# Attention with rotary embedding and two gated MLPs in fp32 on one core: key tails open each P times V accumulation, two P times V groups per pair, issue order of all stages redone

## The chip, the core and the metric

One core of a Trainium2 chip runs the whole program. The metric is device microseconds of one execution. TensorE is called PE here, its weight load PEld, VectorE DVE, ScalarE ACT, GpSimd POOL, SyncE (which issues most DMAs) SP.

## What is computed

The reference, cut to what matters (q, k, v are 4 x 8 x 576 x 64; `rotate` is the rotary embedding):

```python
q_rot, k_rot = (rotate(q), rotate(k))
scores = 1.0 / np.sqrt(D) * np.matmul(q_rot, k_rot.transpose(0, 1, 3, 2))
scores = scores - np.max(scores, axis=-1, keepdims=True)
attn = np.exp(scores)
attn = attn / (np.sum(attn, axis=-1, keepdims=True) + 1e-09)
x = np.matmul(attn, v)          # then heads side by side: 2304 x 512
x = (1.0 / (1.0 + np.exp(-(x @ w_gate))) * (x @ w_val)) @ w_out      # d_ff 1536
h = x @ w_in
return (h * (1.0 / (1.0 + np.exp(-1.702 * h)))) @ w_out2             # d_ff 2048
```

## The kernel before

The program has two stages. The first is attention over 16 pairs of heads (4 batches, 4 pairs each). The second is both MLPs, in chunks of 256 hidden columns; it begins when the last pair's output is there. Numbers keep nearly the whole of fp32: a value is split into a high part and a remainder, and products of both are summed.

For one pair of heads the first stage does this:

- **Load and rope.** `load` (L240) brings q and k of both heads, transposed. `rope_mul` (L275, four multiplications of 128x576, POOL, two of pair 1 on DVE) and `rope_add` (L282, two additions of 128x576, c = 0 and 1) make the rotated values. `split_qk` rounds each half on ACT (L291) and subtracts on DVE (L294); `stack` then copies halves between partitions by six DMAs (L364). Pair 0 has a path of its own (`rope_first`, L266 and L268; PE transposes, L333; copies, L341, L345 and L441). Pair 1 has L316 and L320 in place of L291 and L294.
- **Scores.** `scores` makes nine units of a pair: four row blocks of 128 queries for each of two heads, and one unit of the 64 last queries of both heads (the tail). Each unit is four matmuls of 288 columns (L385, L386), the tail unit four more and six of 64 rows. DVE takes the row maximum from PSUM (`nm`, L388); ACT takes exp with the row sum (`exps`, L403), into tiles P (five buffers) and Pt. Score PSUM has two buffers.
- **Transposes.** `transpose_p` turns P by PE (L457, L467, L472), up to four transposes of 128x128 into one of three PSUM buffers, and copies them to the tile PT on DVE (L441) where the step's number stands in `PT_DVE`, otherwise on ACT (L443).
- **Normalising.** `inverse` sums and inverts (L415, L416 on DVE) and spreads on POOL (L418, L421); `spread` turns that by PE (L428, L430) and copies it to a tile R.
- **P times V.** The queries of a pair are two pieces, a = 0 (256 columns) and a = 1 (320 columns). For each piece `pv` sums over the keys into the one PSUM buffer `ps_x`: for each of four key blocks two matmuls, one for each head, which write 64 partitions each (L488), and one matmul of all 128 partitions for the 64 key tails of both heads (L485, with `vtail`). The profile counts two records for each of these fp32 matmuls. When the sum is closed, DVE multiplies it by R into `xf` (L511). Only then can the next piece open the buffer.

The order of issue is written out by hand. `slot(G)` issues all steps that are due in slot G, and pair i's scores unit u stands in slot 9i + u. The tables before `dec = []` give each step a lag against slot 9i: `PT`, `INV`, `SPREAD`, `PV`, and, counted backwards, `ROPE_MUL`, `ROPE_ADD`, `ROPE_T` and the loads. The last pair has its own row. `slot` also fixes which kind of step comes first within a slot, and `PV_EARLY` names the steps of P times V that stand before the slot's scores. Slots below `FILL` = 20 don't exist: `FIRST` lists the steps of the filling one by one. `DEC` places the decoding of the first weight chunk (L170 to L188), whose high halves are split from raw 8-byte words on ACT, DVE and POOL; `SPLIT` places the splitting of the attention's output (`split_x`, L105 and L106). Each engine works through its own list in order, and a wait holds up all that stands behind it.

In the steady part before the change, a pair's piece a = 0 is issued in two groups of PE work (two key blocks, a scores unit and more, then the two others and the key tails) and piece a = 1 in a third, with its key tails some units later.

Of the kernel before, what the change touches and what calls it, by code (L numbers as in the profile page):

```python
# [31 lines left out]
def attention_then_mlps(  # L32
# [443 lines left out]
    def pv(i, a, ts):  # L476
# [3 lines left out]
        if ts[0] == 0:  # L480
            st[i]["pv"] = ps_t.tile([P, 512], F32, tag="pv", name="ps_x", bufs=1)
        ps = st[i]["pv"]
        for t in ts:
            if t == MAINC:
                nc.tensor.matmul(ps[:, :n], st[i]["vtail"], PT[:, MAINC, :], start=False, stop=True)  # L485
                continue
            for h in range(2):
# [422 lines left out]
```

## Time and profile before

| | |
|---|---|
| three runs | 1144.54, 1144.92 and 1146.52 us, median 1144.92 |
| profiled execution: its own time, its span | 1143.05 us, 1141.0 us |
| busy over the span | PE 98%, PEld 81%, DVE 69%, ACT 37%, POOL 21% |
| attention stage, MLP stage | until about 300 us, from there to the end |
| granted clock of TensorE, mean of the span | 1.000 |

The page of the profile names the share of the span in which each engine is busy, and the chain that ended last: each piece of it is the work that released the next. Where PE's busy time equals the stretch it has no idle time that the records show, though a matmul's end is modelled, so a PE that looks busy can still hide short stalls. The distance from one start to the next is then the better measure. DVE's instructions overlap a little at their ends, so that the sum of their durations can exceed the busy time.

### The profile page before, as it was taken

How to read it: one execution, taken by the hardware profiler on the slowest of the kernel's cores; microseconds unless marked ns; L12 is line 12 of the kernel's file. 1: busy time of each engine (PE TensorE's matmuls, PEld its weight loads, DVE VectorE, ACT ScalarE, POOL GpSimd, SP SyncE). 2: the span in 40 equal slices, each digit the busy share in tenths (PEclk: the TensorE clock that was granted, in tenths of full speed). 3: DMA queues.
4: the chain of work that ended last, by engine and by line, in shares of the span. 5: the costliest groups of instructions: out<-in, count | busy, mean ns of one | idle time of the engine just before them, and what ended most of it. 6: DMA issues, size and time to landing. Idle time of an engine off the chain costs nothing.

```text
span 1141.0 us, 15592 instructions
## 1 busy us (share of the span) xinstructions
PE 1114.4 (98%) x6008; PEld 923.2 (81%) x6008; DVE 785.0 (69%) x1321; ACT 422.6 (37%) x872; POOL 241.0 (21%) x216
## 2 busy tenths in 40 slices
PE   5899999999999999999999999999999999999998
PEld 3677777778788888888888888888888888888887
DVE  5999899897686645656556454666767667676744
ACT  4677777777542211212112123332222222222221
POOL 4544444431331100101001013430101100010100
PEclk9999999999999999999999999999999999999999
DMA  5676656552311111111111010111111111111014
GB/s 175 172 205 153 195 166 171 159 131 52 107 60 38 56 37 38 56 37 54 37 39 46 29 42 34 38 37 37 56 38 41 52 38 37 37 56 38 19 37 129
DMA packets 36409, 85.03 MB, mean 75 GB/s; under 512 B 6640, under 2 KB 11888, under 8 KB 34544
## 3 DMA queue, kind: packets, MB, share of 16 engines
q1 hardware_dynamic: 35232, 83.05, 25.1%
q10 hardware_dynamic: 1104, 1.00, 0.3%
q8 instruction: 47, 0.77, 0.3%
q14 instruction: 26, 0.21, 0.1%
HBM read 60.44 MB, written 4.72 MB: 57 GB/s over the span
## 4 chain that ended last, share of the span: by engine, by line
PE 93%; DVE 5%; ACT 1%; issue 1%; DMA 1%; POOL 0%; ACTq 0%; DVEq 0%
PE psh L519 42%; PE pso L519 30%; PE ps_x L488 5%; PE ps_p L457 4%; PE pss L385 4%; PE pss L386 3%; PE ps_x L485 1%; DVE nm L388 1%; PE psh L541 1%; DVE Y L294 1%; DVE x L282 1%; PE ps_p L472 1%; PE ps_r L428 0%; DVE PT L441 0%; ACT P L403 0%
## 5 line engine op out<-in xcount | busy, mean ns | idle before, releaser
L519 PE MATMUL psh<-xhl,w_in 128*128 128x512 f32 (+1 forms) x2352 | 493.3, 367 | 0.0
L519 PEld LDWEIGHTS psh<-xhl,w_in 128*128 128x128 f32 x2352 | 410.4, 189 | 73.8 <-ACT sg L549 0.2
L549 ACT ACTIVATE sg<-psh 128x512 f32<-128x512 f32 (+1 forms) x140 | 77.6, 554 | 354.2 <-PE psh L519 353.5
L519 PE MATMUL pso<-w_out,g 128*128 128x512 f32 (+1 forms) x870 | 202.5, 388 | 0.0
L519 PEld LDWEIGHTS pso<-w_out,g 128*128 128x128 f32 x870 | 162.1, 188 | 33.1
L551 DVE TENSOR_TENSOR gf<-psh,sg 128x512 f32<-128x512 f32 (+1 forms) x140 | 89.0, 636 | 141.9 <-PE psh L519 95.4
L552 ACT ACTIVATE g<-gf 128x512 fp32r<-128x512 f32 (+1 forms) x140 | 82.5, 589 | 244.6 <-DVE gf L551 242.2
L553 DVE TENSOR_TENSOR g<-gf,g 128x512 fp32r<-128x512 f32 (+1 forms) x140 | 97.3, 695 | 91.8 <-ACT g L552 91.8
L519 PE MATMUL pso<-g,w_out 128*128 128x512 f32 (+1 forms) x720 | 152.8, 368 | 0.0
L519 PEld LDWEIGHTS pso<-g,w_out 128*128 128x128 f32 x720 | 125.8, 189 | 22.6
L188 POOL TENSOR_TENSOR w_in<-wt,w_in 128x512 fp32r<-128x512 f32 x38 | 50.1, 1319 | 370.0 <-DVE w_in L183 362.5
L388 DVE TENSOR_REDUCE nm<-pss 128x1 f32<-128x576 f32 x144 | 108.1, 752 | 25.2 <-PE pss L386 23.2
L403 ACT ACTIVATE P<-pss,nm 128x576 f32<-128x576 f32 x128 | 95.0, 742 | 51.2 <-DVE nm L388 30.9
L275 POOL TENSOR_TENSOR x<-x,rope_sb 128x576 f32<-128x576 f32 x57 | 88.9, 1573 | 71.3 <-DMA x<-in_qk_dram 57.8
L615 DVE TENSOR_TENSOR acc<-pso,acc 128x512 f32<-128x512 f32 (+1 forms) x127 | 83.4, 682 | 20.0 <-PE pso L519 17.7
L188 POOL TENSOR_TENSOR w_out<-wt,w_out 128x512 fp32r<-128x512 f32 x28 | 36.2, 1294 | 267.5 <-DVE w_out L183 265.0
L457 PE MATMUL ps_p<-ident,P 128*128 128x128 f32 x576 | 84.9, 275 | 1.5 <-DVE PT L441 0.8
L598 DVE TENSOR_TENSOR acc<-pso,acc 128x512 f32<-128x512 f32 (+1 forms) x100 | 61.6, 635 | 28.7 <-PE pso L519 28.7
L457 PEld LDWEIGHTS ps_p<-ident,P 128*128 128x128 f32 x576 | 69.4, 143 | 8.6 <-ACT P L403 1.2
L488 PE MATMUL ps_x<-PT,v 128*64 128x320 f32 (+1 forms) x512 | 72.7, 415 | 1.3 <-DVE xf L511 1.3
L443 ACT ACTIVATE PT<-ps_p 128x512 f32<-128x512 f32 (+2 forms) x127 | 62.5, 495 | 5.4 <-PE ps_p L457 2.5
L385 PE MATMUL pss<-X 128*128 128x288 f32 (+3 forms) x176 | 52.3, 323 | 4.3 <-ACT P L403 2.3
(89 smaller groups left out, 1014.7 us busy)
## 6 DMA issues: line engine op xcount, KB each, us to landing
x<-in_qk_dram SPq DMA_DIRECT2D x14, 1152.0 KB, 5.8
raw<-in_moe_w_out_dram SPq DMA_DIRECT2D x28, 512.0 KB, 3.5
raw<-in_moe_w_in_dram SPq DMA_DIRECT2D x16, 512.0 KB, 3.7
raw<-in_moe_w_val_dram SPq DMA_DIRECT2D x12, 512.0 KB, 3.8
raw<-in_moe_w_gate_dram SPq DMA_DIRECT2D x10, 512.0 KB, 3.8
v<-in_v_dram SPq DMA_DIRECT2D x16, 256.0 KB, 5.9
Z<-X SPq DMA_DIRECT2D x14, 288.0 KB, 3.0
Z<-Y SPq DMA_DIRECT2D x14, 288.0 KB, 3.1
```

What stands on the lines that cost most here:

```text
L188: nc.gpsimd.tensor_tensor(w[:, 1, :], f(t), f(w[:, 0, :]), ALU.subtract)
L275: eng.tensor_tensor(x, x, rope_sb[:, t, c * S : (c + 1) * S], ALU.mult)
L385: nc.tensor.matmul(ps[:m, n, o : o + w], T[:, q0 : q0 + m], rhs, start=True, stop=False)
L388: nc.vector.tensor_reduce(nm, ps[:, :, :HALF], axis=AX.XY, op=ALU.max, negate=True)
L403: nc.scalar.activation(st[i]["P"][j][:, c : c + S].rearrange("p (n c) -> p n c", n=2), ps[:, :, :HALF], AF.Exp, bias=nm, accum_out=st[i][" ...
L457: nc.tensor.transpose(ps[:, (2 * x + y) * P : (2 * x + y + 1) * P], st[i]["P"][2 * a + y][:, c * P : (c + 1) * P], ident,)
L488: nc.tensor.matmul(ps[h * D : (h + 1) * D, :n], vt[:, h * MAINC + t, :], PT[:, h * (MAINC + 1) + t, :], start=(t == 0), stop=False,)
L519: nc.tensor.matmul(ps, l(sl, a), r(sr, a), start=(sl == 1 and a == 0), stop=(sl + sr == 0 and a == n - 1))
L551: nc.vector.tensor_tensor(gf, pss[-1][:, :wd], sg, ALU.mult)
L552: nc.scalar.activation(g[:, 0, m, :], gf, AF.Copy)
L553: nc.vector.tensor_tensor(g[:, 1, m, :], gf, f(g[:, 0, m, :]), ALU.subtract)
L615: nc.vector.tensor_tensor(a, ps, a, ALU.add)
```

## The change

All of it is in the tables, in the order within a slot, and in `pv`. In `pv`, the key tails' matmul now opens the accumulation (it carries `start`) and the last key block closes it; before, key block 0 opened and the tails closed. `PV_EARLY` and the lags put all four key blocks of a piece in one slot. The first rope addition of each pair moves from DVE to POOL (`ADD_POOL`). Which copies DVE makes changes (`PT_DVE`, `SPREAD_DVE`): per pair it gives two copies of 128x256 to ACT, takes the two of 64x64 and exchanges the R of 256 columns for the R of 320. Loads, rope, transposes, decodes, splits and the list of the filling are placed anew. No matmul is added or removed.

```diff
-    PT_DVE = (0, 4, 5, 7, 9)
+    PT_DVE = (1, 5, 7, 10)
...
-        if ts[0] == 0:
+        if ts[0] == MAINC:
             st[i]["pv"] = ps_t.tile([P, 512], F32, tag="pv", name="ps_x", bufs=1)
         ps = st[i]["pv"]
         for t in ts:
             if t == MAINC:
-                nc.tensor.matmul(ps[:, :n], st[i]["vtail"], PT[:, MAINC, :], start=False, stop=True)
+                nc.tensor.matmul(ps[:, :n], st[i]["vtail"], PT[:, MAINC, :], start=True, stop=False)
                 continue
             for h in range(2):
                 nc.tensor.matmul(
...
-                    start=(t == 0),
-                    stop=False,
+                    start=False,
+                    stop=(t == MAINC - 1),
                 )
-        if ts[-1] != MAINC:
+        if ts[-1] != MAINC - 1:
             return
...
-    LOAD, LOAD_V, LOAD_VTAIL = 24, 6, 3
-    ROPE_MUL = {ANY: (11, 18, 19, 20)}
-    ROPE_ADD = {ANY: (11, 10)}
+    LOAD, LOAD_V, LOAD_VTAIL = 21, 6, 5
+    ROPE_MUL = {ANY: (15, 14, 12, 11)}
+    ROPE_ADD = {ANY: (13, 10)}
...
-    PT = {ANY: (6, 11, 10, 8, 11, 14, 12, 13, 9, 9, 15, 14), npairs - 1: (6, 7, 13, 12, 10, 10, 12, 17, 13, 18, 11, 10)}
-    INV = {ANY: (11, 9), npairs - 1: (9, 12)}
-    SPREAD = {ANY: (16, 12), npairs - 1: (14, 13)}
-    SPREAD_DVE = (0,)
-    ADD_POOL = ()
+    PT = {ANY: (6, 10, 10, 8, 8, 15, 10, 14, 9, 14, 16, 13), npairs - 1: (6, 8, 11, 13, 8, 14, 19, 21, 12, 18, 14, 10)}
+    INV = {ANY: (9, 11), npairs - 1: (8, 10)}
+    SPREAD = {ANY: (16, 12), npairs - 1: (9, 13)}
+    SPREAD_DVE = (1,)
+    ADD_POOL = (0,)
     LOW_POOL = ()
-    PV_STEPS = [(a, [t]) for a in range(2) for t in range(MAINC + 1)]
-    PV_EARLY = (0, 1, 5, 6, 7, 8)
-    PV = {ANY: (16, 16, 17, 17, 17, 19, 19, 19, 19, 20), npairs - 1: (13, 15, 15, 16, 16, 18, 21, 25, 25, 26)}
-
-    DEC = ((25, 30), (53, 65), (144, 145), (146, 157), (158, 163), (161, 169))
+    PV_STEPS = [(a, [t]) for a in range(2) for t in (MAINC, *range(MAINC))]
+    PV_EARLY = (0,)
+    PV = {ANY: (16, 18, 18, 18, 18, 19, 20, 20, 20, 20), npairs - 1: (14, 17, 17, 17, 17, 21, 23, 23, 27, 28)}
+
+    DEC = ((22, 33), (53, 69), (144, 145), (155, 158), (162, 166), (162, 183))
...
-        for step in (step_pt, step_pv_early, step_scores, step_normalise, step_load, step_pv, step_rope, run_later, step_decode, step_exps, step_spread):
+        for step in (step_pv_early, step_pt, step_scores, step_normalise, step_pv, step_rope, step_load, step_decode, step_spread, run_later, step_exps):
```

Three places show what the tables make of the order.

PE, steady part, before: from the end of a tail scores unit (L386 of 64 rows) on. L488 and L485 are P times V, `x4` are four matmuls.

```order
L386 MATMUL pss<-X,Y 64x288
L488 MATMUL ps_x<-PT_1532,v 64x256 x4
L485 MATMUL ps_x<-PT_1532,vtail_82 128x256
L457 MATMUL ps_p<-ident,P 128x128 x6
L385 MATMUL pss<-X 128x288
L386 MATMUL pss<-X,Y 128x288
L385 MATMUL pss<-X 128x288
L386 MATMUL pss<-X,Y 128x288
L457 MATMUL ps_p<-ident,P 128x128 x4
L488 MATMUL ps_x<-PT_1613,v 64x320 x8
L385 MATMUL pss<-Z 128x288
```

PE, steady part, after, from the group of piece a = 0 on:

```order
L488 MATMUL ps_x<-PT_1522,v 64x256 x8
L457 MATMUL ps_p<-ident,P 128x128 x12
L385 MATMUL pss<-Z 128x288
L386 MATMUL pss<-Z,Zs 128x288
L385 MATMUL pss<-Z 128x288
L386 MATMUL pss<-Z,Zs 128x288
L485 MATMUL ps_x<-PT_1606,vtail_82 128x320
L385 MATMUL pss<-X 128x288
L386 MATMUL pss<-X,Y 128x288
L385 MATMUL pss<-X 128x288
L386 MATMUL pss<-X,Y 128x288
L488 MATMUL ps_x<-PT_1606,v 64x320 x8
```

All eight matmuls of a piece now stand together, followed by transposes or scores, and the tails' matmul stands alone among scores. Over the attention stage the runs of L488 fall from 48 to 34 (from 38 to 26 after pair 5's scores begin). Five of the 48 are followed by a transpose, and 18 of the 34. The tails' matmul is followed by scores 13 times, before never.

DVE, steady part, before, around the multiplication L511 that frees `ps_x` from piece a = 0 (L282 rope additions, L294 the low halves, L388 row maxima):

```order
L388 TENSOR_REDUCE nm<-pss 128x1 x2
L282 TENSOR_TENSOR x<-x 128x576
L441 COPY R_2441<-ps_r 128x256
L388 TENSOR_REDUCE nm<-pss 128x1
L282 TENSOR_TENSOR x<-x 128x576
L511 TENSOR_TENSOR xf_1468<-ps_x,R_2441 128x256
L294 TENSOR_TENSOR Y<-x,X 128x576 x2
```

DVE, the same place after:

```order
L388 TENSOR_REDUCE nm<-pss 128x1 x2
L282 TENSOR_TENSOR x<-x 128x576
L294 TENSOR_TENSOR Y<-x,X 128x576 x2
L388 TENSOR_REDUCE nm<-pss 128x1
L415 TENSOR_SCALAR r<-sum 128x4
L416 RECIPROCAL r<-r 128x4
L511 TENSOR_TENSOR xf_1467<-ps_x,R_2655 128x256
```

One L282 has gone to POOL, and both L294 now stand ahead of L511.

POOL, one pair of the steady part, before (L275 rope multiplications, L418 and L421 the inverted sums):

```order
L418 COPY w<-r 128x256
L421 TENSOR_SCALAR w_1418<-block,r 128x128
L275 TENSOR_TENSOR x<-x,rope_sb 128x576
L418 COPY w<-r 128x256
L275 TENSOR_TENSOR x<-x,rope_sb 128x576 x3
```

POOL, one pair after:

```order
L418 COPY w<-r 128x256 x2
L421 TENSOR_SCALAR w_1456<-block,r 128x128
L275 TENSOR_TENSOR x<-x,rope_sb 128x576 x2
L282 TENSOR_TENSOR x<-x 128x576
L275 TENSOR_TENSOR x<-x,rope_sb 128x576 x2
```

The rope work of a pair stands in one run behind both copies of the inverted sums, with the addition in its middle.

## Rows read from the trace of the kernel before

**Rows 1.** Busy time by stretch: us, then PE, PEld, DVE, ACT, POOL (instructions), PE clock, DMA

```profile
15.00:33.00 18.00, 12.40 (x52) 9.93 (x50) 13.48 (x18) 12.28 (x28) 12.43 (x9) 1.00 0.26 90
33.00:103.00 70.00, 65.91 (x489) 52.23 (x490) 66.03 (x113) 49.76 (x120) 32.20 (x31) 1.00 0.67 190
...
169.00:283.00 114.00, 114.00 (x867) 91.14 (x865) 97.47 (x176) 84.05 (x203) 39.85 (x42) 1.00 0.50 130
300.00:1141.00 841.00, 836.89 (x3990) 705.42 (x3988) 529.00 (x875) 214.48 (x381) 117.47 (x92) 1.00 0.15 46
```

**Rows 2.** The chain in order of time, steady part: start, us, what

```profile
226.21 0.54 PE ps_x L485 x2
...
242.64 0.54 PE ps_x L485 x2
```

**Rows 3.** The same chain, around a decode

```profile
141.18 0.54 PE ps_x L485 x2
141.72 0.44 PE ps_p L457 x4
...
176.76 0.54 PE ps_x L485 x2
```

**Rows 4.** PE in order of time, tail scores and half a group: start, us

```profile
234.28 0.29 PE L386 MATMUL pss<-Z,Zs 128*128 128x288 f32 x1
234.41 0.19 PE L385 MATMUL pss<-X 128*64 128x64 f32 x1
...
234.87 0.29 PE L386 MATMUL pss<-X,Y 128*64 128x288 f32 x1
235.09 1.08 PE L488 MATMUL ps_x<-PT,v 128*64 128x256 f32 x8
236.10 0.70 PE L485 MATMUL ps_x<-PT,vtail 128*128 128x256 f32 x2
236.64 0.82 PE L457 MATMUL ps_p<-ident,P 128*128 128x128 f32 x6
```

**Rows 5.** PE in order of time, the group of the other part

```profile
188.89 2.37 PE L488 MATMUL ps_x<-PT,v 128*64 128x320 f32 x16
191.20 0.40 PE L385 MATMUL pss<-Z 128*128 128x288 f32 x1
191.43 0.30 PE L386 MATMUL pss<-Z,Zs 128*128 128x288 f32 x1
```

**Rows 6.** PE in order of time, a group followed by a transpose

```profile
289.44 0.33 PE L467 MATMUL ps_p<-ident,Pt 128*128 128x128 f32 x1
289.61 0.70 PE L485 MATMUL ps_x<-PT,vtail 128*128 128x320 f32 x2
```

**Rows 7.** DVE in order of time, pair 8, decode pieces among it

```profile
149.55 1.92 DVE L282 TENSOR_TENSOR x<-x 128x576 f32<-128x576 f32 x1
151.40 1.89 DVE L180 SCALAR_TENSOR_TENSOR spare<-spare 128x512 uint32<-128x512 uint32 x1
...
154.21 0.74 DVE L282 TENSOR_TENSOR x<-x 128x576 f32<-128x576 f32 x1
154.87 0.41 DVE L511 TENSOR_TENSOR xf<-ps_x,R 128x256 f32<-128x256 f32 x1
```

**Rows 8.** PE's wait that follows on it

```profile
155.34 0.49 PE L488 MATMUL ps_x<-PT,v 128*64 128x320 f32 x2 [1.01 <-DVE xf L511]
```

**Rows 9.** Groups of instructions, two steady pairs, DVE and POOL: count, busy, mean ns

```profile
L388 DVE TENSOR_REDUCE nm<-pss 128x1 f32<-128x576 f32 x18 | 13.5, 752 | 3.5 <-PE pss L386 3.2
L282 DVE TENSOR_TENSOR x<-x 128x576 f32<-128x576 f32 x4 | 4.8, 1194 | 0.0
...
L275 POOL TENSOR_TENSOR x<-x,rope_sb 128x576 f32<-128x576 f32 x9 | 14.3, 1595 | 10.5 <-DMA x<-in_qk_dram 10.5
```

**Rows 10.** The start in order of time, POOL and PE

```profile
7.14 1.40 POOL L268 TENSOR_TENSOR first<-first 128x576 f32<-128x576 f32 x1
...
16.96 0.61 PE L386 MATMUL pss<-X,Y 128*128 128x288 f32 x1 [1.37 <-ACT Y L443]
```

More of the change, by code (lines that the diff above doesn't have):

```diff
@@ L647, in attention_then_mlps @@
-    DEC = ((25, 30), (53, 65), (144, 145), (146, 157), (158, 163), (161, 169))
-    SPLIT = {(0, 0): 124, (0, 1): 152, (0, 2): 141, (0, 3): 145, (1, 0): 162, (1, 1): 155, (1, 2): 144, (1, 3): 1001}
+    PT = {ANY: (6, 10, 10, 8, 8, 15, 10, 14, 9, 14, 16, 13), npairs - 1: (6, 8, 11, 13, 8, 14, 19, 21, 12, 18, 14, 10)}
[3 more added lines that the diff above has]
+    ADD_POOL = (0,)
+    LOW_POOL = ()
+    PV_STEPS = [(a, [t]) for a in range(2) for t in (MAINC, *range(MAINC))]
@@ L649, in attention_then_mlps @@
+    PV_EARLY = (0,)
+    PV = {ANY: (16, 18, 18, 18, 18, 19, 20, 20, 20, 20), npairs - 1: (14, 17, 17, 17, 17, 21, 23, 23, 27, 28)}
+    DEC = ((22, 33), (53, 69), (144, 145), (155, 158), (162, 166), (162, 183))
+    SPLIT = {(0, 0): 90, (0, 1): 157, (0, 2): 151, (0, 3): 117, (1, 0): 1005, (1, 1): 996, (1, 2): 151, (1, 3): 1000}
     EARLY = (999, 999, 999, 999, 999, 999, 999, 999, 999, 999, 999, 999)
     FILL = 20
[L651 removed]
@@ new lines, in attention_then_mlps @@
+    FIRST = (('rm', 0, 0, 1), ('rm', 0, 1, 0), ('rm', 0, 4, 0), ('rm', 0, 3, 0), ('ld', 2), ('rm', 0, 2, 1), ('ra', 0, 0), ('t0', 0, 2), ('hi', 0, 2), ('t0', 0, 0), ('t0', 0, 1), ('rm', 0, 5, 1), ('ra', 0, 1), ('lo', 0, 2), ('st', 0, 2, 0, 1), ('lv', 0), ('hi', 0, 0), ('t0', 1, 1), ('t0', 1, 0), ('hi', 0, 1), ('hi', 1, 1), ('rm', 1, 0, 0), ('st', 0, 0, 0, 0), ('t0', 1, 2), ('lo', 0, 1), ('hi', 1, 0), ('st', 0, 1, 0, 0), ('lo', 1, 1), ('lo', 0, 0), ('rm', 1, 1, 0), ('st', 1, 0, 0, 1), ('st', 0, 0, 1, 1), ('lo', 1, 0), ('hi', 1, 2), ('rm', 1, 2, 0), ('st', 1, 0, 1, 0), ('lo', 1, 2), ('st', 1, 1, 1, 0), ('st', 0, 2, 1, 0), ('sc', 0, 0), ('st', 1, 1, 0, 1), ('ex', 0, 0), ('sc', 0, 1), ('ex', 0, 1), ('rm', 1, 3, 1), ('ra', 1, 0), ('rm', 2, 0, 0), ('sc', 0, 3), ('ra', 1, 1), ('sc', 0, 2), ('ex', 0, 3), ('sh', 1, 0, 0), ('sl', 1, 0, 1, 1), ('rm', 2, 1, 0), ('ex', 0, 2), ('sh', 1, 1, 0), ('sc', 0, 5), ('sc', 0, 7), ('sh', 0, 0, 0), ('sl', 0, 0, 0, 1), ('ex', 0, 5), ('sh', 0, 1, 0), ('pt', 0, 2, 1), ('pt', 0, 1, 1), ('ex', 0, 7), ('st', 0, 1, 1, 1), ('sc', 0, 4), ('sl', 0, 1, 0, 0), ('sl', 1, 0, 0, 1), ('sc', 0, 8), ('sl', 1, 1, 0, 0), ('lt', 0), ('sh', 1, 0, 1), ('ex', 0, 4), ('no', 0, 0), ('sc', 0, 6), ('ra', 2, 0), ('pt', 0, 0, 1), ('ex', 0, 8), ('sd', 1, 1), ('ex', 0, 6), ('rm', 2, 3, 0), ('sd', 1, 0), ('sc', 1, 0), ('ld', 3), ('pt', 0, 4, 1), ('pt', 0, 10, 0), ('sc', 1, 1), ('rm', 2, 2, 0), ('pt', 0, 9, 1), ('ex', 1, 0), ('rm', 3, 2, 0), ('rt', 2, 0), ('pt', 0, 3, 0), ('sc', 1, 3), ('sp', 2, 0), ('lv', 1), ('ex', 1, 1), ('rm', 3, 3, 0), ('ra', 2, 1), ('pt', 0, 7, 0), ('ex', 1, 3), ('pt', 0, 6, 1), ('sc', 1, 2), ('rt', 2, 1), ('pt', 0, 8, 0), ('ex', 1, 2), ('pv', 0, 0), ('sp', 2, 1), ('pv', 0, 1), ('pv', 0, 2), ('sc', 1, 5), ('no', 0, 1), ('pv', 0, 3), ('ex', 1, 5), ('pt', 0, 5, 0), ('sc', 1, 6), ('sc', 1, 4), ('rm', 3, 1, 0), ('rs', 0, 0, 1), ('ex', 1, 6), ('ex', 1, 4), ('ld', 4), ('lt', 1), ('pv', 0, 4), ('ra', 3, 1), ('rm', 3, 0, 1), ('lv', 2), ('rs', 0, 1, 0), ('sc', 1, 7), ('ex', 1, 7), ('sc', 1, 8), ('pt', 1, 3, 1), ('ex', 1, 8), ('pt', 1, 0, 0), ('pt', 1, 6, 1), ('sc', 2, 1), ('xs', 0, 0), ('ra', 3, 0), ('pt', 0, 11, 0), ('pt', 1, 4, 1), ('rt', 3, 0), ('pt', 1, 8, 1), ('sp', 3, 0), ('pt', 1, 2, 1), ('sc', 2, 0), ('ex', 2, 1), ('rt', 3, 1), ('pv', 0, 5), ('sp', 3, 1), ('ex', 2, 0), ('pt', 1, 1, 0), ('no', 1, 0))
```

1 line of the change is left out of this document (removed).

## The prediction

> **What bounds the kernel now.** I read the busy times by stretch first. From 300 us on, in the MLP stage, PE is busy for 836.89 of 841 us, and what is missing is the end of the program [rows 1]. The change leaves the MLP's matmuls as they are, so time can come from the attention stage alone. There three parts differ. From 15 to 33 us PE has 5.6 us of idle time, from 33 to 103 us 4.1 us, with DVE busy for 66.03 of 70 us: the filling waits on DVE. From 169 to 283 us PE is busy for all of 114 us [rows 1]. The chain of waits says the same: in the steady part its pieces are PE's own, and a pair takes 242.64 - 226.21 = 16.43 us [rows 2]. Around the decode, two pairs take 176.76 - 141.18 = 35.58 us, 2.7 us more than twice that [rows 3].
>
> A PE that shows no idle time still spends time between matmuls, which the timeline shows as distances between starts. Scores follow each other at 0.13 us, and the first 64-row matmul of the tail unit also starts 0.13 us after the matmul before it [rows 4]. But from the last of those to the first L488 it takes 0.22 us: 0.09 us for entering. From an L488 group to the second scores matmul it costs too: the first takes 0.23 us [rows 5] where 0.13 is usual, so 0.10 us for leaving. Inside, eight records of 256 columns take 1.01 us [rows 4], sixteen of 320 columns 2.31 us [rows 5]. Two equations for a price per column and a fixed part give 0.42 ns and 0.14 us. Entering, fixed part and leaving are **0.33 us for each run of L488**. The tails' matmul behind a group pays the leaving price as well: its two records of 256 columns take 0.54 us [rows 4], as long as two of 320 columns elsewhere [rows 2]. A single transpose behind one takes 0.17 us [rows 6], where four take 0.44 us [rows 3], so leaving to a transpose costs only 0.06 us.
>
> **The change, part by part.**
>
> *Groups.* Of 48 runs of L488, 34 remain. Twelve of the 14 that go lie after 103 us, where PE is the bound: 12 x 0.33 = 4.0 us off the path. The two in the filling I leave to the term for it.
>
> *Leaving.* Runs followed by a transpose grow from 5 to 18: 13 x (0.10 - 0.06) = 0.5 us less.
>
> *The tails' matmul ahead of scores*, 13 times, is not in the trace. Bounds: nothing, as the step into the tail scores [rows 4], to 0.10 us each, as leaving L488 [rows 5]: 0 to 1.3 us. It uses the whole array like the scores, so I take nothing.
>
> *The first rope addition on POOL.* DVE loses one of its two L282 per pair, 0.74 us when nothing disturbs it [rows 7], 1.19 us in the mean [rows 9]. POOL gains one more operation like its L275 of 1.6 us, beside 10.5 us of waiting in two pairs [rows 9]. In the steady part this is off the path and I count nothing for it; PE is the cover. If POOL were late, DVE's second L282, then L294, the stacking DMAs on SP and the next pair's scores would wait. On SP the load of x now stands behind the loads of v and the tails; its lag of 21 slots is 6 ahead of the first rope multiplication, some 11 us at 16.43 / 9 us a slot. Copies exchanged between DVE and ACT are under half a microsecond each and count nothing, for the same cover.
>
> *The decode.* Its 2.7 us came when DVE fell behind: an L282 of 1.92 us and a decode piece of 1.89 us followed each other, L511 ended late [rows 7], and PE waited 1.01 us to open the next piece [rows 8]. The same operations remain, four slots later, with DVE about 1 us a pair freer. Bounds 0 and 2.7; I take -1.7 us.
>
> *The filling.* Up to pair 5 DVE sheds six L282, 4.4 to 7.2 us of work by the two durations above, in a stretch where PE idles 4.1 us [rows 1]. It cannot gain much more than that, and the new list may also waste it: bounds -4.8 (with the two groups) to +2; I take -2.0. At the very start the cosine multiplication on POOL, 1.40 us [rows 10], goes to DVE, and the first full scores matmul, which waited 1.37 us for an ACT copy to Y [rows 10], finds that copy first in ACT's new list: -1.0 us, between -2.0 and +1.
>
> *New waits.* The tails' matmul of a = 1 now opens `ps_x` and must wait for L511 of a = 0, and DVE has two L294 ahead of that L511. From the end of the tail unit PE has 0.44 (four transposes), 0.52 (a scores unit), 0.09, 0.14 + 16 x 256 x 0.42 ns = 1.87, 12 x 0.11 + 0.06 = 1.38 (transposes) and 0.52: 4.8 us. DVE has in that time two L388 of 0.75 [rows 9], L282 and two L294 at 0.74 each (one shape, the price of [rows 7]) and L511 of 0.41: 4.1 us, and besides two small operations, the hand-overs, and what shows of the ACT rounding between L282 and the second L294. This is on the edge. Behind a late opening stand the scores, and behind them DVE and ACT. I take 0.12 us for each of 13 pairs, +1.5 us, between 0 and 0.5 each.
>
> Sum: -4.0 - 0.5 - 1.7 - 2.0 - 1.0 + 1.5 = **-7.7 us** against the profiled execution's 1143.05 us (its span of 1141.0 and 2.05 us around it): 1135.35. The median of the three runs stands 1.87 us above that execution, so I forecast 1137.2 us.
>
> **Rivals.**
>
> *The opening waits as a rule.* If the DVE list above ends 0.5 us late in every pair, 13 x 0.5 = 6.5 us, 5.0 more than counted: 1142.2 us. For it: the sum of both sides is equal, and [rows 8] shows such a wait once. Against: PE's queue of scores is what DVE waits for elsewhere, and DVE is lighter. Chance 0.13.
>
> *POOL blocks DVE (slower).* An L282 of 1.92 us stands beside one of 0.74 us of the same shape [rows 7]; the long one ran while POOL was at work on L275. If POOL's run, now five operations of 1.4 to 1.6 us, still goes on when DVE reaches its L282 and L294, each can be held 1.2 us. One such hit in every pair makes the opening 1.2 us late, 13 x 1.2 = 15.6 us, 14.1 more than counted: 1151.3 us. Against: that run now follows the inverted sums, which DVE makes at and after L511, so it has most of a pair's 16.4 us for about 8 us of work. It decides when POOL needs more than about 14 us from L418 to its last L275. Chance 0.06. The Trainium skill, page "SBUF — State Buffer", section "Who interferes with whom", says that a DVE instruction with two SBUF inputs and a GpSimd one that reads SBUF exclude each other for the whole instruction. By that rule moving an addition to POOL gives DVE one more to collide with; it gives no other time than this rival's.
>
> *Grouping buys nothing.* If the price belonged to the change between 128x128 and 128x64 matmuls and not to L488, then the old group behind the tail unit, itself 128x64, would have had no entry of its own, and the tail unit followed by transposes would pay now what L488 paid: three round trips before, three after. The first two terms go: 1137.2 + 4.5 = 1141.7 us. Against it: the tail unit is entered at 0.13 us, without a price, and L488 behind it still pays 0.09 [rows 4]. Chance 0.06. The Trainium skill, page "TensorEngine Tiling (Array Packing)", section "Key Properties", says that changing the tiling mode, not just the tile, drains TensorE; that rule predicts this rival. The trace agrees for L488 and not for the tail unit.
>
> *The new filling is worse.* If the first 103 us cost 2 us more instead of 3 less: 1142.2 us. The list is new throughout, which the old trace cannot judge. Chance 0.10.
>
> **How the numbers follow.** The forecast has 0.65. Its own bounds run from -4.0 - 0.5 - 2.7 - 4.8 - 2.0 = -14.0 (1130.9) to about -3 (1142). I give 1131.5 to 1142.0: it holds the forecast, the grouping rival and about half of the first and last rival, and leaves out the slow one. About 0.2% (2.3 us) is what a measurement can tell from no change, so faster means under 1142.6 us. That takes 0.64 of the forecast, 0.07 of the first rival, 0.06 of the grouping rival and 0.05 of the last: 0.82. The rest of these is within 0.2%, with little beyond: 0.10 the same, 0.08 slower.
>
> **What would show it.** Right: in the steady part a pair takes about 16.2 us (16.43 less 0.33 and 0.04 of leaving, plus 0.12 of waiting), L488 appears as runs of 16 records, a 256-column run takes about 1.87 us, the tails' matmul stands at 0.13 us from its scores, the first L385 behind it is not long, two pairs around the decode take less than 34 us, and the MLP begins near 292 us. Wrong: L485 of 320 columns with an idle time released by L511 in each pair (first rival), L282 or L294 on DVE near 1.9 us in each pair (second), 64-row scores followed by slow transposes (third), pair 5's scores after 103 us (fourth).

## The result, and the profile after

The changed kernel takes **1134.62 us** (median of four runs, 1133.15 to 1134.97) against 1145.31 us for the kernel before (four runs, 1144.54 to 1146.52): a ratio of 0.9903, with a 95% interval from 0.9886 to 0.992. The forecast was 1137.2 us, its range 1131.5 to 1142.0. The profiled execution has a span of 1131.0 us, 10.0 less than before.

Busy time by stretch of the changed kernel, in the columns of [rows 1]:

```profile
15.00:33.00 18.00, 14.04 (x61) 11.32 (x60) 16.66 (x26) 12.25 (x27) 10.65 (x9) 1.00 0.35 116
33.00:97.00 64.00, 61.86 (x468) 50.53 (x467) 54.74 (x103) 48.61 (x117) 35.94 (x34) 1.00 0.72 204
162.00:259.00 97.00, 97.00 (x753) 79.87 (x752) 76.40 (x152) 74.89 (x178) 43.12 (x45) 1.00 0.59 151
290.00:1131.00 841.00, 836.83 (x3990) 705.57 (x3988) 529.64 (x877) 214.35 (x381) 117.44 (x92) 1.00 0.15 46
```

The MLP is as long as before, so the whole gain lies in the attention stage. In the filling PE's idle time is halved (2.14 of 64 us, before 4.09 of 70 [rows 1]), and DVE has room there: 54.74 of 64 us, where it had 66.03 of 70. In the steady part PE still has no idle time.

The chain in order of time (start, us, what), its L485 of 320 columns:

```profile
133.81 0.54 PE ps_x L485 x2
...
149.79 0.34 DVE xf L511
150.18 0.81 PE ps_x L485 x2
...
166.78 0.54 PE ps_x L485 x2
...
182.91 0.54 PE ps_x L485 x2
...
199.08 0.54 PE ps_x L485 x2
```

From 182.91 to 199.08 a steady pair takes 16.17 us, where it took 16.43 [rows 2]. Two pairs around the decode take 166.78 - 133.81 = 32.97 us, where they took 35.58 [rows 3]. L511 shows in the chain at 149.79, where the opening tail had to wait for it. That is the first rival, and in the whole program it happens only at the two decodes (85.08 and 150.18 us).

PE in order of time, a steady pair of the changed kernel:

```profile
211.27 1.95 PE L488 MATMUL ps_x<-PT,v 128*64 128x256 f32 x16
213.15 1.53 PE L457 MATMUL ps_p<-ident,P 128*128 128x128 f32 x12
...
214.91 0.30 PE L386 MATMUL pss<-Z,Zs 128*128 128x288 f32 x1
215.05 0.70 PE L485 MATMUL ps_x<-PT,vtail 128*128 128x320 f32 x2
215.35 0.54 PE L385 MATMUL pss<-X 128*128 128x288 f32 x1
215.72 0.29 PE L386 MATMUL pss<-X,Y 128*128 128x288 f32 x1
...
223.16 0.59 PE L485 MATMUL ps_x<-PT,vtail 128*128 128x256 f32 x2
223.59 0.27 PE L467 MATMUL ps_p<-ident,Pt 128*128 128x128 f32 x1
223.66 0.40 PE L385 MATMUL pss<-Z 128*128 128x288 f32 x1
...
226.24 0.29 PE L386 MATMUL pss<-X,Y 128*64 128x288 f32 x1
226.38 0.60 PE L457 MATMUL ps_p<-ident,P 128*128 128x128 f32 x4
```

The run of sixteen 256-column records takes 213.15 - 211.27 = 1.88 us. From the start of the 320-column tail to the second scores matmul it takes 215.72 - 215.05 = 0.67 us, which is 0.54 for the tail [rows 2] and the usual 0.13: the tail goes over to scores for nothing. The tail unit goes over to transposes in 0.14 us. Both were taken as free. The opening tail itself starts 0.14 us behind the scores ahead of it (214.91 to 215.05), the usual spacing, so it waits for nothing here.

DVE and POOL in the filling, groups by shape, from pair 1's first scores to pair 5's. First the kernel before (33.47 to 102.86 us), then the changed one (32.48 to 96.86):

```profile
L294 DVE TENSOR_TENSOR Y<-x,X 128x576 fp32r<-128x576 f32 x8 | 10.4, 1319 | 0.0
L282 DVE TENSOR_TENSOR x<-x 128x576 f32<-128x576 f32 x10 | 9.5, 948 | 0.1
L275 POOL TENSOR_TENSOR x<-x,rope_sb 128x576 f32<-128x576 f32 x17 | 26.9, 1594 | 19.5 <-DMA x<-in_qk_dram 19.4
```

```profile
L294 DVE TENSOR_TENSOR Y<-x,X 128x576 fp32r<-128x576 f32 x8 | 7.2, 907 | 0.1
L282 DVE TENSOR_TENSOR x<-x 128x576 f32<-128x576 f32 x4 | 4.2, 1052 | 0.0
L275 POOL TENSOR_TENSOR x<-x,rope_sb 128x576 f32<-128x576 f32 x17 | 24.3, 1450 | 0.0
```

DVE sheds 5.3 us of L282 (five of the six went to POOL, one fell out of the stretch) and, without losing one, 3.2 us of L294. Over the whole attention stage before, 29 of DVE's 58 L282 and L294 overlapped a POOL instruction; those took 1.25 us (L282) and 1.59 us (L294) in the mean, the others 0.75. Now 3 of 43 overlap one. POOL no longer waits for x, which the prediction had seen as 10.5 us in two steady pairs [rows 9]. In two steady pairs (194.43 to 226.73 us) nothing on DVE is slowed any more:

```profile
L294 DVE TENSOR_TENSOR Y<-x,X 128x576 fp32r<-128x576 f32 x4 | 3.0, 754 | 0.2
L282 POOL TENSOR_TENSOR x<-x 128x576 f32<-128x576 f32 x2 | 2.8, 1419 | 0.2
...
L282 DVE TENSOR_TENSOR x<-x 128x576 f32<-128x576 f32 x2 | 1.5, 748 | 0.0
```

An L282 took 1194 ns in the mean before [rows 9]; the one left takes 748. DVE is thus relieved of 2.4 - 0.75 = 1.65 us a pair, where the prediction counted about one.

### The profile page after: what moved, and what is told of

It reads as the page before. It is cut to its first block, busy times and chain, and to the rows that moved or that the text cites. A ratio compares the mean times of both kernels' runs of the same rounds, so it can differ in the third digit from the quotient of the medians.

```text
span 1131.0 us, 15601 instructions
## 1 busy us (share of the span) xinstructions
PE 1109.5 (98%) x6008; PEld 925.3 (82%) x6008; DVE 756.4 (67%) x1312; ACT 423.4 (37%) x866; POOL 252.2 (22%) x231
## 4 chain that ended last, share of the span: by engine, by line
PE 95%; DVE 3%; DMA 1%; ACT 1%; issue 0%; POOL 0%; ACTq 0%; DVEq 0%; POOLq 0%
PE psh L519 43%; PE pso L519 30%; PE ps_x L488 5%; PE ps_p L457 5%; PE pss L385 4%; PE pss L386 3%; PE ps_x L485 1%; PE psh L541 1%; PE ps_r L428 1%; PE ps_p L472 1%; DVE nm L388 1%; DVE Y L294 0%; DMA first<-in_cos_dram 0%; DVE x L282 0%; PE ps_r L430 0%
## 5 line engine op out<-in xcount | busy, mean ns | idle before, releaser
L519 PEld LDWEIGHTS pso<-w_out,g 128*128 128x128 f32 x870 | 162.1, 188 | 33.1
L388 DVE TENSOR_REDUCE nm<-pss 128x1 f32<-128x576 f32 x144 | 108.5, 754 | 29.7 <-PE pss L386 28.6
L275 POOL TENSOR_TENSOR x<-x,rope_sb 128x576 f32<-128x576 f32 x58 | 82.1, 1436 | 3.0 <-DMA x<-in_qk_dram 2.9
L457 PE MATMUL ps_p<-ident,P 128*128 128x128 f32 x576 | 78.9, 277 | 0.0
L457 PEld LDWEIGHTS ps_p<-ident,P 128*128 128x128 f32 x576 | 66.3, 142 | 8.1 <-issue 6.3
L488 PE MATMUL ps_x<-PT,v 128*64 128x320 f32 (+1 forms) x512 | 69.6, 412 | 0.0
```

The costliest lines, as they stand in the source:

```text
L275: eng.tensor_tensor(x, x, rope_sb[:, t, c * S : (c + 1) * S], ALU.mult)
L388: nc.vector.tensor_reduce(nm, ps[:, :, :HALF], axis=AX.XY, op=ALU.max, negate=True)
L457: nc.tensor.transpose(ps[:, (2 * x + y) * P : (2 * x + y + 1) * P], st[i]["P"][2 * a + y][:, c * P : (c + 1) * P], ident,)
L488: nc.tensor.matmul(ps[h * D : (h + 1) * D, :n], vt[:, h * MAINC + t, :], PT[:, h * (MAINC + 1) + t, :], start=False, stop=(t == MAINC - 1),)
L519: nc.tensor.matmul(ps, l(sl, a), r(sr, a), start=(sl == 1 and a == 0), stop=(sl + sr == 0 and a == n - 1))
```

## The experiments

Times are medians. The kernel before was timed beside each set: 1144.13 us beside the first four runs, 1145.0 beside the next, 1144.97 beside the last. "Step" is the time from a pair's first scores to the next pair's in the steady part (before 16.43, changed 16.15). The changed kernel's 1134.62 us stood beside 1145.31, so a comparison with it crosses sets in which the kernel before differs by up to 1.2 us. Profiled executions lie up to 2.4 us from their kernel's median, and every figure from inside a run is of one execution.

**1. Grouping alone.** The kernel before, with the two half groups of piece 0 in one slot (34 runs of L488; tails still close, all else old).

```diff
-    PV_EARLY = (0, 1, 5, 6, 7, 8)
-    PV = {ANY: (16, 16, 17, 17, 17, 19, 19, 19, 19, 20), npairs - 1: (13, 15, 15, 16, 16, 18, 21, 25, 25, 26)}
+    PV_EARLY = (5, 6, 7, 8)
+    PV = {ANY: (17, 17, 17, 17, 17, 19, 19, 19, 19, 20), npairs - 1: (13, 15, 15, 16, 16, 18, 21, 25, 25, 26)}
```

> The kernel before with one change: the two key blocks of piece a = 0 that stood one scores unit earlier join the other two, so that the runs of L488 fall from 48 to 34; the key tails still close, everything else stands as before. Theory (each run costs 0.33 us on PE, wherever it stands): 14 runs fewer, 4.6 us less over the attention stage, 16.1 us a pair in the steady part instead of 16.43, the time 4 to 5 us under the kernel before. Rival (the price belongs to the tiling change as such, so that the run behind the 64-row tail scores had none of its own and nothing is saved): 16.43 us a pair and no change within 1 us. Rival (PE's shorter list only turns into waits on DVE, which keeps both rope additions): 16.3 to 16.4 us a pair, less than 2 us saved.

Measured: 1151.99 us, ratio 1.0065 [1.005, 1.008]: slower. The step is 17.09 us. PE in order of time, where it waits in each pair:

```profile
219.24 0.38 PE L385 MATMUL pss<-Z 128*128 128x288 f32 x1
...
220.86 0.29 PE L386 MATMUL pss<-X,Y 128*128 128x288 f32 x1
221.75 0.40 PE L385 MATMUL pss<-Z 128*128 128x288 f32 x1 [0.59 <-ACT P L403]
```

0.33 us a run should be saved (run 3 below measures 0.30), and 1.0 us of waits is the price. The scores at 221.75 need the PSUM buffer that the scores at 219.24 began to fill, and exp gives it back only 2.51 us later.

**2. Both additions on DVE.** The changed kernel with `ADD_POOL = ()`.

> The changed kernel with the first rope addition of each pair back on DVE; all else as changed. Theory (the filling gained 6 us because DVE has six rope additions fewer there): pair 5's scores begin 3 to 6 us later than at 96.9 us, the steady pairs stay within 0.1 us of 16.15 or wait for L511, the time 4 to 7 us above the changed kernel. Rival (the new list of the filling gained it by its order): pair 5's scores begin within 1 us of 96.9 us and the time is within 1.5 us of the changed kernel.

Measured: 1150.14 us, ratio 1.005 [1.0035, 1.0065], 15.5 us above the changed kernel. Pair 5's first scores come at 101.16 us instead of 96.86: 4.3 us of the filling. But the step is 17.65 us, 1.5 above, where about nothing was expected. In order of time, POOL, DVE and PE:

```profile
214.57 5.54 POOL L275 TENSOR_TENSOR x<-x,rope_sb 128x576 f32<-128x576 f32 x4
218.99 1.74 DVE L282 TENSOR_TENSOR x<-x 128x576 f32<-128x576 f32 x1
221.38 0.66 PE L457 MATMUL ps_p<-ident,P 128*128 128x128 f32 x4 [0.38 <-DVE PT L441]
```

An L282 beside POOL's multiplications takes 1.74 us instead of 0.75, the copies behind it come late, and PE waits. This is the mechanism of the second rival, but it acts on the addition that was put back on DVE; the L282 that the changed kernel leaves there takes 0.75 us here too (at 207.43 us). The addition on POOL, for which the prediction counted nothing in the steady part, carries that part too. In the filling (32.81 to 101.16 us) L294 is as free here as in the changed kernel, although DVE keeps both additions:

```profile
L294 DVE TENSOR_TENSOR Y<-x,X 128x576 fp32r<-128x576 f32 x8 | 6.6, 834 | 0.1
```

So it is freed by the new places of POOL's work and not by the addition that moved.

**3. Three groups again.** The changed kernel with piece 0 split over two slots (47 runs).

```diff
-    PV = {ANY: (16, 18, 18, 18, 18, 19, 20, 20, 20, 20), npairs - 1: (14, 17, 17, 17, 17, 21, 23, 23, 27, 28)}
+    PV = {ANY: (16, 17, 17, 18, 18, 19, 20, 20, 20, 20), npairs - 1: (14, 17, 17, 17, 17, 21, 23, 23, 27, 28)}
```

> The changed kernel with the key blocks of piece a = 0 split again, two of them one slot earlier: 47 runs of L488 instead of 34, the 13 new ones followed by transposes. Theory (0.29 us for a run that leaves to a transpose): 13 x 0.29 = 3.8 us more, about 16.45 us a pair instead of 16.15. Rival (the tiling change as such is the price): the new runs stand behind the 64-row tail scores and cost no entry, 0 to 1.5 us more in all.

Measured: 1138.17 us, ratio 0.9948 [0.9933, 0.9962]; its span is 3.9 us above the changed kernel's, its step 16.45, 0.30 above. With 13 runs more that is 0.30 us a run. The prediction's parts give 0.29 for a run that is left to a transpose (0.33 less 0.04), and the third rival (grouping buys nothing) falls.

**4. The addition on POOL alone.** The kernel before with `ADD_POOL = (0,)`, old distances.

> The kernel before with the first rope addition of each pair on POOL; all else as before. Theory (DVE bounds the filling and the decode): pair 5's scores begin 2 to 4 us earlier than at 102.9 us, the decode around pair 8 loses 1 to 2 us of its 2.7, the steady pairs stay at 16.43, the time 3 to 6 us under the kernel before. Rival (POOL and DVE block each other, since POOL's run of rope work in the old order coincides with DVE's L294): L294 on DVE near 1.9 us more often, no gain or a loss up to 5 us.

Measured: 1154.88 us, ratio 1.0099 [1.0082, 1.0117]: slower; step 17.17. In order of time, POOL and ACT:

```profile
226.09 1.42 POOL L275 TENSOR_TENSOR x<-x,rope_sb 128x576 f32<-128x576 f32 x1 [5.41 <-DMA x<-in_qk_dram]
227.46 1.93 POOL L282 TENSOR_TENSOR x<-x 128x576 f32<-128x576 f32 x1
...
229.43 1.26 ACT L291 ACTIVATE X<-x 128x576 fp32r<-128x576 f32 x2 [2.41 <-POOL x L282]
```

POOL gets x late, adds late, ACT stands 2.41 us in front of its rounding with the exps behind it, and PE waits for score buffers. Pair 5's scores begin at 105.73 us, 2.9 us later, where 2 to 4 us earlier were expected, and the loss is twice the rival's.

**5. The addition on POOL at its new distances.** The kernel before, with

```diff
-    LOAD, LOAD_V, LOAD_VTAIL = 24, 6, 3
-    ROPE_MUL = {ANY: (11, 18, 19, 20)}
-    ROPE_ADD = {ANY: (11, 10)}
+    LOAD, LOAD_V, LOAD_VTAIL = 21, 6, 3
+    ROPE_MUL = {ANY: (15, 14, 12, 11)}
+    ROPE_ADD = {ANY: (13, 10)}
...
-    ADD_POOL = ()
+    ADD_POOL = (0,)
```

The list of the filling loses three multiplications of pair 4, which the loop now issues.

> The kernel before with the Q half's rope addition on POOL and, unlike the run in which that was done alone, with the changed kernel's distances for the rope multiplications (15, 14, 12, 11), additions (13, 10) and the x load (21); the 48 runs of P times V and all other distances stay. My theory now: the addition on POOL failed in the old list only because it lay too near its readers, and P times V in three groups still costs 0.3 us a run. Then the steady step is back at 16.4 us, the filling gains part of the 4.3 us that the addition is worth there (pair 5 starts at 82 to 85 us, against 85.66 before), and the time is 1139 to 1144 us. Rival: the old list has other places that are too tight for a later addition; then the steps stay at 16.8 us or more and the time is above 1148 us.

Measured: 1140.13 us, ratio 0.9956 [0.9942, 0.997]. The step is 16.43 us, as expected, with no waits. (The 82 to 85 us in the expectation belong to pair 4, whose scores began at 85.66 before; here they begin at 85.92, as the first pair came out 1.9 us later in the profiled execution.) From pair 1's first scores to pair 5's it takes 66.98 us, before 69.39: -2.4. The two pairs of the decode take 34.08, before 35.58: -1.5. So the addition on POOL with the rope work at its new places gives 4.9 us without any grouping, nearly half of the change. The new places without the addition on POOL were not run on the kernel before.

**6. The same, and grouping.** Run 5 with the edit of run 1.

> The run above, and P times V of piece 0 also moved to one slot (34 runs instead of 48, key tails still close the accumulation). My theory: with one addition less on DVE the copies of the transposed probabilities are in time again, so that the grouping, which alone in the old list was turned into 1.0 us of waits a pair, now pays its 0.3 us a pair: steady step 16.1 to 16.2 us, time 4 to 5 us under the run above, 1134 to 1140 us. Rival: what the old list lacks for the grouping is the new places of the transposes and copies (their distances and which engine copies), not DVE's 0.75 us; then waits of 0.5 us or more a pair are left, the step is 16.4 us or more and the time is that of the run above or more.

Measured: 1149.34 us, ratio 1.0039 [1.0024, 1.0054], 9.2 us above run 5. The rival held: the step is 17.08 us, with the wait of run 1. First PE of run 5, then of run 6, at the same place of a pair:

```profile
212.74 0.29 PE L386 MATMUL pss<-X,Y 128*128 128x288 f32 x1
212.96 1.08 PE L488 MATMUL ps_x<-PT,v 128*64 128x256 f32 x8
213.98 0.40 PE L385 MATMUL pss<-Z 128*128 128x288 f32 x1
```

```profile
217.76 0.38 PE L385 MATMUL pss<-Z 128*128 128x288 f32 x1
...
219.38 0.29 PE L386 MATMUL pss<-X,Y 128*128 128x288 f32 x1
220.26 0.40 PE L385 MATMUL pss<-Z 128*128 128x288 f32 x1 [0.59 <-ACT P L403]
```

In run 5 the half group stands between two scores units. Take it away and the second comes before its buffer is free: 220.26 - 217.76 = 2.50 us from scores to scores of one buffer, as in run 1. DVE is not late here. It takes the maximum of the scores of 217.76 (the last matmul ends at 218.55) at once, and ACT follows at once:

```profile
218.58 0.76 DVE L388 TENSOR_REDUCE nm<-pss 128x1 f32<-128x576 f32 x1
...
219.38 0.74 ACT L403 ACTIVATE P<-pss,nm 128x576 f32<-128x576 f32 x1
```

L488 was work and **spacer** at once.

**7. Tails close again.** The changed kernel with each tail behind its own run.

```diff
-    PV_STEPS = [(a, [t]) for a in range(2) for t in (MAINC, *range(MAINC))]
-    PV_EARLY = (0,)
-    PV = {ANY: (16, 18, 18, 18, 18, 19, 20, 20, 20, 20), npairs - 1: (14, 17, 17, 17, 17, 21, 23, 23, 27, 28)}
+    PV_STEPS = [(a, [t]) for a in range(2) for t in range(MAINC + 1)]
+    PV_EARLY = ()
+    PV = {ANY: (18, 18, 18, 18, 18, 20, 20, 20, 20, 20), npairs - 1: (17, 17, 17, 17, 17, 23, 23, 27, 28, 28)}
```

In `pv`, `start` and `stop` stand as in the kernel before. One step of P times V goes from the list of the filling to the loop.

> The changed kernel with each key tail put back behind its own run of P times V, where it closes the accumulation (33 runs; tails at distances 18 and 20, last pair 17 and 28); everything else of the changed kernel stays. My theory: what pays is the number of runs, not the place of the tail, since the price of a run is paid once on leaving it, whether to a tail's matmul or to scores: the time is that of the changed kernel, 1134.6 us within 1.5 us, the steady step 16.15 us; at the two decodes, where the opening tail waited 0.42 us for VectorE, up to 0.8 us may come back. Rival: the opening tail is what saves (leaving a run to a tail's matmul is dearer than leaving it to scores, or the tail's lone matmul was the cost): then up to 0.1 to 0.3 us for each of 31 runs returns, 3 to 9 us, 1138 us or more.

Measured: 1139.88 us, ratio 0.9955 [0.994, 0.997], 5.3 us above the changed kernel. The time is the rival's, the reason is neither's. PE, where the 256-column tail was gone:

```profile
226.17 0.38 PE L385 MATMUL pss<-Z 128*128 128x288 f32 x1
...
228.22 0.27 PE L467 MATMUL ps_p<-ident,Pt 128*128 128x128 f32 x1
228.73 0.40 PE L385 MATMUL pss<-Z 128*128 128x288 f32 x1 [0.24 <-ACT P L403]
```

A single transpose now takes 0.51 us to the next scores, where it took 0.07 (223.59 to 223.66 above): 0.44 us of the step's 0.48. In the changed kernel the tail's 0.43 us stand there, between two scores units. Behind its run it is no spacer.

**8. Both additions on POOL.** The changed kernel with `ADD_POOL = (0, 1)`.

> The changed kernel with the second rope addition (the K half) on POOL as well. My theory: in the steady part of the changed kernel VectorE no longer sets the time, so its further 0.75 us a pair are worth nothing there, while the K half's addition stands at distance 10 right behind the multiplication on POOL at 11 and takes 1.4 us there instead of 0.75; ScalarE's rounding and VectorE's subtraction of that half then come some 1 to 2 us late in their slot. The step rises by 0 to 0.7 us and the time is 1135 to 1146 us. Rival: VectorE is still the limit of the filling (27.9 us busy of 31.5 between 32.5 and 64 us), and relief there is worth another 2 to 4 us: 1130 to 1133 us.

Measured: 1134.37 us, ratio 0.9905 [0.989, 0.992]: the changed kernel's time. The step stays at 16.15 to 16.16 in most pairs, so DVE no longer sets it. The two pairs of the decode take 32.37 us instead of 32.96, but pair 1 takes 18.51 instead of 16.45. The time lies between the two expected ranges, and neither theory had this pair of effects. Why pair 1 is longer was not taken apart; run 7 has a long pair 1 too (17.72 us) without this addition.

**9. Grouping at the new places.** Run 5 with piece 0 at distance 18 and piece 1 at 20, tails closing, old distances of all else.

```diff
-    PV_EARLY = (0, 1, 5, 6, 7, 8)
-    PV = {ANY: (16, 16, 17, 17, 17, 19, 19, 19, 19, 20), npairs - 1: (13, 15, 15, 16, 16, 18, 21, 25, 25, 26)}
+    PV_EARLY = ()
+    PV = {ANY: (18, 18, 18, 18, 18, 20, 20, 20, 20, 20), npairs - 1: (13, 15, 15, 16, 16, 18, 21, 25, 25, 26)}
```

Four steps of P times V go from the list of the filling to the loop, here and in run 10.

> The kernel before with the Q half's addition on POOL at the new distances and P times V in two groups, as in the run that came out at 1149.34 us with 1.07 us of waits a pair, but with the two groups at the changed kernel's places: piece 0 at distance 18 behind a pair's first scores, piece 1 at 20 behind its third, key tails closing; all other distances old. My theory now: a run of L488 is also a spacer. There are two PSUM buffers for scores, and one comes back about 2.5 us after its scores began (0.79 us of scores, 0.76 of row maximum, 0.74 of exponential, and what lies between); taking the 1.0 us run from between the 7th and the 8th scores left these too close, and PE waited 0.75 us there. With the groups behind the first and the third scores the rest of the scores are crowded less, so that the waits fall to 0.5 us a pair or less: step 16.1 to 16.6 us, against 17.08, and 1134 to 1142 us. Rival: the waits come from copies of VectorE and ScalarE that the old distances put too close, wherever the runs stand; then the step stays at 16.9 us or more and the time at 1147 us or more.

Measured: 1153.13 us, ratio 1.0075 [1.006, 1.0091]; step 17.06. My expectation missed. The wait stands exactly where it stood in run 6 (2.49 us from scores to scores of one buffer): moving the groups elsewhere puts nothing into the gap that they leave. The rival's number held; its cause, late copies, is not what PE waits for there.

**10. The same without relief.** Run 9 with both additions on DVE at the old rope distances.

> The same without the addition on POOL: the kernel before with P times V in two groups at distances 18 and 20 (both additions on VectorE, old rope distances). It asks how much of the gain the grouping brings without VectorE's relief. My theory (spacing sets the steady waits, relief of VectorE matters in the filling and around the decodes): steady step within 0.1 us of the run above, and a time 2 to 6 us above it, 1138 to 1146 us. Rival: without the relief VectorE is late in each pair; then the step is 0.3 us or more above that of the run above and the time above 1146 us.

Measured: 1161.63 us, ratio 1.0148 [1.0129, 1.0167]: the rival. On top of the wait of run 9 comes one behind DVE in most pairs (steps of 17.06 to 19.03 us). DVE and PE:

```profile
214.33 2.64 DVE L294 TENSOR_TENSOR Y<-x,X 128x576 fp32r<-128x576 f32 x2
218.95 0.40 PE L385 MATMUL pss<-X 128*128 128x288 f32 x1 [0.69 <-ACT P L403]
```

**11. Tails open, nothing else.** The kernel before with each tail directly ahead of its first run.

```diff
-    PV_STEPS = [(a, [t]) for a in range(2) for t in range(MAINC + 1)]
+    PV_STEPS = [(a, [t]) for a in range(2) for t in (MAINC, *range(MAINC))]
-    PV_EARLY = (0, 1, 5, 6, 7, 8)
-    PV = {ANY: (16, 16, 17, 17, 17, 19, 19, 19, 19, 20), npairs - 1: (13, 15, 15, 16, 16, 18, 21, 25, 25, 26)}
+    PV_EARLY = (0, 1, 2, 5, 6, 7, 8, 9)
+    PV = {ANY: (16, 16, 16, 17, 17, 19, 19, 19, 19, 19), npairs - 1: (13, 13, 15, 15, 16, 18, 18, 21, 25, 25)}
```

In `pv`, `start` and `stop` stand as in the changed kernel. The list of the filling loads pair 0's tails earlier and holds one step of P times V more; the runs of L488 are 49.

> The kernel before with one part of the change alone: each key tail opens its accumulation, directly ahead of its first run of P times V, instead of closing it; three groups stay (some 48 runs), as does everything else. My theory: the place of the tail is worth only what it does to the two slots it leaves and enters: leaving a run of L488 for a tail cost 0.05 us more than leaving it for transposes, so up to 0.1 us a pair comes back, and the 320-column tail, now next to its run, no longer stands alone between two scores as 0.54 us of spacing, which may give a wait of up to 0.4 us a pair. Time 1143 to 1150 us. Rival: opening is what saves by itself; then the step falls by 0.2 us or more and the time is under 1142 us.

Measured: 1152.08 us, ratio 1.0067 [1.0052, 1.0082]; step 16.83. Opening by itself saves nothing. The 320-column tail no longer stands between two scores units, and four transposes, which take 0.36 us to the next scores where PE need not wait, take 0.70 there:

```profile
214.39 0.60 PE L457 MATMUL ps_p<-ident,P 128*128 128x128 f32 x4
215.09 0.40 PE L385 MATMUL pss<-Z 128*128 128x288 f32 x1
```

That is 0.34 us of waiting, and before the scores after these come 0.13 more. And here the first rival costs more: the opening tail waits 1.0 us for L511 at each of the two decodes, and 0.38 us once outside them (243.84 us). At the second decode:

```profile
158.70 0.81 PE L485 MATMUL ps_x<-PT,vtail 128*128 128x320 f32 x2 [1.02 <-DVE xf L511]
```

**12. Second addition on POOL from pair 4 on.** The changed kernel, filling untouched.

```diff
-        (nc.gpsimd if c in ADD_POOL else nc.vector).tensor_tensor(x[:, 0], x[:, 0], x[:, 1], ALU.add)
+        (nc.gpsimd if c in ADD_POOL or i > 3 else nc.vector).tensor_tensor(x[:, 0], x[:, 0], x[:, 1], ALU.add)
```

> The changed kernel with the second rope addition (K half) on POOL too, but only from pair 4 on, so that the filling stays as it is. With both additions on POOL in all pairs the opening tails no longer waited 0.42 us for VectorE at the two decodes and the decode at pair 8 cost 0.6 us less, while pair 1 took 2 us more. My theory: the first stays and the second goes: MLP matmuls begin 0.5 to 1 us earlier than in the changed kernel (289.59 us), and the time is 1133 to 1134.6 us, too close to tell for certain. Rival: the 2 us of pair 1 came from run to run and not from the addition; then the time is that of both additions on POOL, 1134.4 us, and the filling of this run differs by as much either way.

Measured: **1132.74 us** (1132.1 to 1134.32), ratio 0.9898 [0.9884, 0.9913]. Pair 1 takes 16.45 us again, the MLP begins at 288.96 us instead of 289.59, and the opening tail at the decode no longer waits:

```profile
149.50 0.29 PE L386 MATMUL pss<-Z,Zs 128*128 128x288 f32 x1
149.63 0.70 PE L485 MATMUL ps_x<-PT,vtail 128*128 128x320 f32 x2
149.93 0.54 PE L385 MATMUL pss<-X 128*128 128x288 f32 x1
```

The time is just under the expected range. It is the fastest kernel of the study, but its interval overlaps that of the changed kernel, and pair 1 is one execution of each kernel.

## Why the prediction was right, and where it was not

The attention stage by the first scores of its pairs, in the two profiled executions:

| from, to | before | after | difference |
|---|---|---|---|
| start, pair 1 | 33.47 | 32.48 | -1.0 |
| pair 1, pair 5 | 69.39 | 64.38 | -5.0 |
| pairs 5 and 6 | 32.89 | 32.30 | -0.6 |
| pairs 7 and 8 (decode) | 35.58 | 32.96 | -2.6 |
| pairs 9 to 14 | 98.74 | 97.01 | -1.7 |
| pair 15, first matmul of the MLP | 29.36 | 30.46 | +1.1 |

One thing is shifted in it: the run of piece 0 (1.88 us) stood ahead of a pair's first scores and now stands behind them. That counts for 1.9 us too much in the second row and comes back in the last. With it, the terms are:

- **Groups and leaving** (predicted -4.0 - 0.5 = -4.5): 10 pairs at 0.29 are -2.9, and the last row less the shift is -0.8: -3.7. The price of a run is right (run 3), but a steady pair gives 0.28 us where 0.33 + 0.04 was counted. Where the other 0.09 us of a pair went was not taken apart.
- **New waits** (predicted +1.5, 0.12 us in each pair): nothing in the steady pairs. The opening tail waits at the decodes alone, and that is in the next term. So the steady 16.15 us, where "about 16.2" was said, is in part luck: of its two terms the gain was counted 0.09 us too high and the wait 0.12 us too high.
- **The decode** (predicted -1.7): -2.6 less two steady gains of 0.29, so -2.0. Run 5 shows that -1.5 of it comes with the addition on POOL and the new rope distances.
- **The filling** (predicted -2.0, with two groups): -5.0 + 1.9 = -3.1. Run 5 gives -2.4 without grouping; two groups of 0.33 make up the rest. The term was 1.1 us too small. It counted DVE's shed additions against PE's visible idle time, and neither the L294 that the new places of POOL's work free (3.2 us, above) nor the end of POOL's waiting for x. Which of these brought the 1.1 us is not shown; freeing L294 is not enough by itself, since in run 2 it is free too and this stretch takes 68.34 us: 1.05 less than before, of which the shift alone is 1.9.
- **The very start** (predicted -1.0): -1.0, but not by the first scores, which come at 15.23 us instead of 15.00; the first pair behind them is 1.2 us shorter. That the size fits is luck: pair 1's scores begin at 33.4 to 35.7 us in the eight profiled kernels with the old list of the start and at 32.0 to 33.1 in the six with the new one, 1.8 us apart in the mean.

They sum to -9.8, predicted -7.7: the waits that did not come (1.5), the filling (1.1) and the decode (0.3) brought more than counted, the groups 0.8 less. What was expected of the profile came out: sixteen records, 1.88 us, free tails, under 34 us around the decode. The MLP begins at 289.59, 2.4 us before the time given.

The rivals: *opening waits* happens at the two decodes alone, about 0.4 us each; why it did not become the rule is not shown. In run 2, with both additions on DVE, it stays at the decodes as well, beside other waits, and in run 11 it comes in one pair more. *POOL blocks DVE* does not happen in the steady part: of POOL's five operations the last two begin at 222.48 us and take 2.80, and DVE's L282 begins at 227.25. *Grouping buys nothing* is refuted by run 3. *The new filling is worse* is refuted by 96.86 us for pair 5.

**What the prediction did not see** is that its terms can't be had one by one. It subtracted 0.33 us for each run as if the rest stayed, and counted nothing for the addition on POOL in the steady part with PE as the cover. Done alone, grouping costs 7.9 us (run 1), the addition on POOL 10.8 (run 4), the opening tails 7.1 (run 11). Two conditions were missing from its steps. First, the new order has no room on DVE for the second addition in any pair, not only in the filling: with it there the changed kernel is slower than the one before (run 2), and run 10 waits for DVE in most pairs. Second, a scores unit can't begin until some 2.5 us after the scores two units earlier, so the PE work between units is spacing; the prediction checked the order for late inputs, never for this distance. What in the changed kernel keeps it is the 256-column tail alone in a slot (run 7), which can stand there, two slots ahead of its run, only because it opens, and the transposes at their new distances. That these transposes matter was argued from runs 6 and 9, where the old ones leave the gap; no run moved them alone.

In sum: 4.9 us come with the addition on POOL at the new rope distances (run 5), some 3.6 with the last grouping (run 3 against the changed kernel; 4.7 if each is set against the kernel before of its own set), and what remains, 1 to 2, lies between runs 5 and 3 and was not taken apart.

## What to carry to other kernels

On an engine that is always busy, a run with an entry and exit price is worth merging, but look first at what it separated: measure how long a buffer takes from its first write to its return, and check that distance at every place the merge empties. Work that can be placed freely (here an accumulation's odd member, moved to its head) is the filler for such a gap. Before calling an engine's load hidden, add to it what its instructions lose beside another engine, and try the change's parts alone: parts that each cost time can gain together.

## What the runs showed of the hardware that was not expected

- Matmuls that use half the array are not alike. The tail scores (128*64 in the rows, as L488) are entered at 0.13 us [rows 4] and left for transposes at 0.14 us; runs of L488 cost 0.30 us each to enter and leave, measured whole (run 3). The Trainium skill, page "TensorEngine Tiling (Array Packing)", section "Key Properties", says that a change of the tiling mode drains TensorE. The runs agree for L488 and show no such price for the tail scores; what sets the two apart was not tried.
- On DVE, L282 took 1.74 us beside POOL's L275 (run 2) and 0.75 alone, L294 1.32 in the mean of the filling before and 0.75 in the steady part after, while L388, which reads PSUM, kept 0.75 us in both kernels. The Trainium skill, page "SBUF — State Buffer", section "Who interferes with whom", says that only the port pair shared by VectorE and GpSimd causes contention, as an exclusive lock; these numbers agree. The size was the surprise: 3.2 us of L294 in four pairs, with as many L294 as before, where POOL's work was moved in time; run 2, with no addition moved to POOL, shows the same.
